# Order of the opening, block 0's transposes in two steps, and a new plan for the rest of a fused attention and feed-forward kernel

## The chip, the cores and the metric

The kernel runs on one core of a Trainium2 chip. A core has five engines that run on their own and wait for each other through semaphores: TensorE (PE, matmuls; PEld is its weight load, which overlaps), VectorE (DVE), ScalarE (ACT), GpSimd (POOL) and SyncE (SP, which here only issues DMA transfers). The metric is the device time of one execution in microseconds; lower is better. A chip's run of the same kernel repeats within some tenths of a per cent.

## The reference

The input x has 2048 rows of 576 columns in bf16. All of it is one layer with two branches that share a layer norm:

```
xn = layernorm(x)
q, k, v = split(xn @ wqkv)              # 32 heads of 18 columns
p = softmax(mask(q @ k.T * 18**-0.5))   # a row sees itself and the 255 rows before it
s = (p @ v) @ wo
h = sigmoid(xn @ w_gate) * (xn @ w_up)  # 4608 columns
g = silu(h @ w_down)
out = x + s * g
```

## The kernel before

**Tiles and stages.** The rows are worked in four stages (chunks) of 512 rows, each of four blocks of 128. In a stage: layer norm of the blocks, transposed copy `xnT` (columns on partitions), the query and key projection (`build_qk`), v (`build_v`), scores, exp and mask per head group (`build_attn`), probabilities times v (`build_pv`), output projection (`build_wo`), gate and up products for 36 tiles of 128 feed-forward columns (`gate_up` in `build_ffn`), their tanh and multiply (`tail`), and the down product (`down`). 576 columns are 64 + 4 x 128: `xnT` has five column blocks, of which block 0 holds the first 64 columns twice (the "doubled columns": `ln:dup`, L561, copies them next to the normalised row). All matmuls run in pairs on the two halves of TensorE's rows, by the helper `pair` (L127): one 64-row product for gate, one for up, at the same time. A gate/up tile has a first half of four column blocks (`f10`, 8 matmuls) and a second half of five (`f11`, 10 matmuls, which need the doubled block and the remainder weights `wgr`).

**The opening.** In stage 0 x comes by four DMAs of 144 KB (`load_x`) on SP's queue, ahead of the first weights: gate and up of the first group of two tiles (`wgs`, 256 KB each), their remainders (`wgr`, 64 KB each), the next group, and so on. Block by block, `build_ln` does the statistics on DVE (L541 to L547; for the third block on ACT, L600 to L604), the power for 1/sqrt on POOL (L549), the normalise (L557) and the doubled copy (L561) on DVE, ten small transposes on TensorE (L613) into PSUM and one evacuating copy to `xnT` (L590; on ACT for blocks 0 to 2, on DVE for block 3, `XE_ENG`). While TensorE has no data, `warm` gives it products of zeros: 43 pairs of 128 columns at the start and ten after the first transposes (`NWARM`). The first two gate/up tiles (`NEARLY = 2`) are done in four parts of one block each (`PARTS`), so that they can start when block 0 is there.

**What sets the order.** Nothing is ordered by hand. `build_graph` lists operations with their dependences, engine, estimated duration and priority. `schedule` is a list planner: it walks through a modelled time, and on each engine takes next the operation with the earliest modelled start (plus 10 ns per priority step), takes PSUM units for it from pools (`pool_s`, `pool_f`, `pool_v`), and so fixes each engine's instruction order; `emit` writes it out with semaphore waits. On the chip each engine keeps that order whatever the real times are. Constants such as `SPACE_NS` (least distance of score products), `DMA_ISSUE_NS` and the DMA slack model the chip.

**Runs.** `build_pv` makes eight runs of products of probabilities with v (L817), two per stage: 384 instructions in some 2.3 us (256 in stage 0). TensorE's instructions come from memory in blocks of 256. `fits` lets a run start only where, by the plan's times, the block boundaries in it have `FETCH_NS` between an instruction 320 places ahead and the boundary; otherwise the run is put off.

Of the kernel before, what the change touches and what calls it, by code (L numbers as in the profile page):

```python
# [7 lines left out]
S = 2048  # L8
D = 576
# [36 lines left out]
FETCH_NS = (6200.0, 4350.0)  # L46
RUN_NS = 6.3
STEP_NS = (54.0, 30.6)
# [21 lines left out]
X_PRIO = (0, 0, 0, 0)  # L70
# [4 lines left out]
XE_ENG = ("ACT", "ACT", "ACT", "DVE")  # L75
NWARM = (43, 10)
NEARLY = 2
FIRST_SLACK_NS = (-800.0, -1500.0)
BUSY_SLACK_NS = 1500.0
PARTS = (((0, 1), (1, 2), (2, 3), (3, 4)),) * NEARLY  # L80
# [10 lines left out]
POOL_IN_NS = 140.0  # L91
DMA_PE_NS = 690.0
FILL_NS = 100.0
SPACE_NS = (1700, 1800, 1700, 1700)
# [62 lines left out]
class Pool:  # L157
# [12 lines left out]
    def pick(self, n, now, barred=()):  # L170
        free = []
        for u in self.units:
            if u in barred:
                continue
            h = self.last[u]
            if h is None:
                free.append((0.0, self.units.index(u), u))
            elif h.rel and all(r.idx >= 0 for r in h.rel):
                free.append((max(now, max(r.end for r in h.rel) + self.late), self.units.index(u), u))
# [4 lines left out]
        return max(g[0] for g in got), sorted(g[2] for g in got)  # L184
# [11 lines left out]
class Op:  # L196
    __slots__ = ("eng", "est", "deps", "fn", "name", "prio", "start", "end", "tok", "needs_tok",
                 "nbytes", "slack", "idx", "succs", "cidx", "odeps", "acq", "lane", "filler", "space", "ni", "run", "then")

    def __init__(self, eng, est, fn, name, deps, prio, nbytes, odeps, acq):  # L200
# [33 lines left out]
        self.then = None  # L234
        for d in self.odeps:
# [23 lines left out]
class Builder:  # L259
# [40 lines left out]
    def alloc_memory(self):  # L300
# [61 lines left out]
        self.pool_f = Pool("F", [2, 3, 1], last)  # L362
        self.pool_v = Pool("V", [0, 1, 2, 3], last)

    def build_graph(self):
# [16 lines left out]
        self.op_xnT = [[] for _ in range(NC)]  # L382
        self.op_v = {}
# [34 lines left out]
    def load_x(self, c, i=0):  # L418
        if c == 0:
            for i in range(BPC):  # L420
                self.x_dma[i] = (self.dma(self.x0[:, i, :], self.x[i * P:(i + 1) * P, :], P * D * 2, f"dma:x{i}", ("x0", i), prio=X_PRIO[i]),
                                 self.x0[:, i, :])
                self.x_dma[i][0].slack = -220.0
# [20 lines left out]
    def load_rem(self, dst, srcs, name, lane, prio, deps=()):  # L444
        return [self.dma(dst[ROWS[1 - t], :], src[0:RD, :], RD * src.shape[1] * 3, name, lane + (t,), deps=deps, prio=prio)
                for t, src in enumerate(srcs)]

    def build_consts(self):
# [15 lines left out]
        self.warm(NWARM[0], z, None, 107)  # L464
# [25 lines left out]
    def warm(self, n, dep, before, est):  # L490
        h, zero = self.warm_h, self.warm_src

        def f_warm(eng):
            return pair(eng, self.halves(h, P), lambda r, t: zero[r, :],
                        lambda r, t: zero[r, :], True, True)
        for i in range(n):
            w = self.op("PE", est, f_warm, f"warm:{i}", deps=[dep], prio=4, acq=None if before else h, odeps=[before], ni=4)
            w.filler = h
            h.release(w)
            before = w  # L500
# [24 lines left out]
    def build_ln(self, c):  # L525
# [3 lines left out]
        for i in range(BPC):  # L529
# [49 lines left out]
            h = self.pool_s.hold()  # L579

            def f_tr(eng, h=h, sn=sn):
                return self.transposes(eng, h, lambda r, o: self.xnr[r, sn, o:o + P])
# [759 lines left out]
```

## Time and profile before

| what | us |
|---|---|
| median of three runs | 556.4 (556.1 to 556.68) |
| the profiled execution's own time | 556.48 |
| its span, first to last instruction | 555.2 |
| TensorE busy | 549.9 |
| first gate/up product starts | 7.98 |
| last TensorE work ends | 552.7 |

TensorE is the full engine, so idle time of the others costs nothing by itself. Times in the views count from the span's start. In a row of the timeline the first number is the start, the second the length of the group, xN the number of instructions in it; in brackets stand the idle time before it and what ended it. A pair of matmuls of n columns takes n / 2.4 + 2.7 ns at the full pace: 56 ns for 128 columns, 216 ns for 512.

### The profile page before, as it was taken

What the parts mean: (1) busy time and instruction counts of PE and PEld (TensorE: products, weight loads), DVE (VectorE), ACT (ScalarE), POOL (GpSimd) and SP (SyncE); (2) the same over time, 40 slices, a digit from 0 to 9 for tenths busy, and PEclk for the clock granted to TensorE, in tenths of its full rate; (3) what the DMA queues carried; (4) which work ended last, traced back from release to release, by engine and by line L of the source; (5) the groups of instructions that cost most, each with busy time, mean ns of one, the idle gap of its engine ahead of it and who ended that gap; (6) DMA issues with size and microseconds to landing.
All of it is one profiled execution on the core that took longest, in us unless ns stands there. A gap on an engine that the chain in (4) does not pass through costs nothing.

```text
span 555.2 us, 19412 instructions
## 1 busy us (share of the span) xinstructions
PE 549.9 (99%) x8342; PEld 341.2 (61%) x8342; DVE 325.1 (59%) x782; ACT 271.7 (49%) x379; POOL 208.8 (38%) x360
## 2 busy tenths in 40 slices
PE   8999999999999999999999999999999999999998
PEld 7454455777555655577855565447877655445887
DVE  5467677745966545746565557664455657653511
ACT  4246554432566543645265563764165555765021
POOL 5634353826271230554452322745063332700300
DMA  8899999542256664462126653663013464540001
GB/s 230 234 263 239 248 241 257 150 91 59 72 164 182 198 167 132 129 161 53 32 65 193 201 162 101 185 179 87 9 34 103 119 204 138 153 134 2 20 28 46
DMA packets 141213, 75.87 MB, mean 137 GB/s; under 512 B 43676, under 2 KB 139260, under 8 KB 141128
## 3 DMA queue, kind: packets, MB, share of 16 engines
q1 hardware_dynamic: 133704, 68.71, 47.3%
q0 software_dynamic: 7424, 5.92, 4.0%
q8 instruction: 66, 1.08, 0.8%
q14 instruction: 19, 0.16, 0.1%
HBM read 63.18 MB, written 2.36 MB: 118 GB/s over the span
## 4 chain that ended last, share of the span: by engine, by line
PE 98%; DMA 1%; SPq 0%; issue 0%; DVE 0%; ACT 0%
PE ps L127 95%; PE ps L817 3%; DMA wgs<-in_B_w_up_dram 1%; SPq L290 0%; ACT thf L1087 0%; PE ps L613 0%; DVE thf L1089 0%; DVE xf L1092 0%
## 5 line engine op out<-in xcount | busy, mean ns | idle before, releaser
L127 PE MATMUL ps<-xnT,wgs 64*128 64x512 bf16 (+1 forms) x2400 | 284.0, 368 | 0.6 <-DMA wgs<-in_B_w_up_dram 0.5
L767 ACT ACTIVATE expr<-ps 128x1024 bf16<-128x1024 f32 (+4 forms) x160 | 155.0, 968 | 81.0 <-PE ps L127 80.5
L127 PEld LDWEIGHTS ps<-xnT,wgs 64*128 64x128 bf16 x2400 | 114.7, 94 | 108.6 <-issue 1.1
L127 PE MATMUL ps<-wd_sb,hT 64*128 64x288 bf16 (+2 forms) x2448 | 152.7, 276 | 0.0
L290 POOL DMA_DIRECT2D qk<-qd x160 | 82.9, 524 | 161.7 <-PE ps L127 152.9
L977 DVE SCALAR_TENSOR_TENSOR hT<-tring,ps 128x512 bf16<-128x512 bf16 x144 | 98.6, 685 | 74.2 <-ACT tring L974 72.6
L974 ACT ACTIVATE tring<-ps 128x512 bf16<-128x512 f32 x144 | 86.2, 598 | 113.9 <-PE ps L127 112.3
L127 PEld LDWEIGHTS ps<-wd_sb,hT 64*128 64x128 bf16 x2448 | 113.0, 94 | 29.4
L780 DVE TENSOR_TENSOR expr<-expr,mask 128x128 bf16<-128x128 bf16 (+2 forms) x240 | 65.2, 299 | 62.0 <-ACT expr L767 59.4
L290 POOL DMA_DIRECT2D oT<-o2T x72 | 36.8, 520 | 115.3 <-DVE ot L848 52.4
L731 POOL TENSOR_SCALAR kx<-kprev,small 128x256 bf16<-128x256 bf16 x64 | 60.1, 949 | 6.0 <-PE ps L127 5.1
L127 PE MATMUL ps<-qk,kx 64*128 64x320 bf16 (+1 forms) x704 | 59.2, 254 | 0.0
L127 PE MATMUL ps<-xnT,wgr 64*128 64x512 bf16 (+1 forms) x300 | 56.0, 367 | 0.0
L127 PEld LDWEIGHTS ps<-qk,kx 64*128 64x128 bf16 x704 | 31.9, 94 | 26.6
L127 PE MATMUL ps<-xnT,wqg 64*128 64x512 bf16 (+1 forms) x320 | 37.7, 355 | 0.0
L652 DVE CAST qd<-ps 128x1024 bf16<-128x1024 f32 (+1 forms) x20 | 22.3, 1115 | 11.1 <-PE ps L127 11.1
L845 DVE STREAM_TRANSPOSE ot<-ps 128x512 f32<-128x512 f32 x32 | 20.3, 687 | 13.9 <-PE ps L817 13.8
L127 PEld LDWEIGHTS ps<-xnT,wgr 64*128 64x128 bf16 x300 | 15.0, 94 | 16.4
L731 DVE TENSOR_SCALAR kx<-qk,small 128x512 bf16<-128x512 bf16 x64 | 21.9, 370 | 5.4 <-PE ps L127 4.9
L853 DVE STREAM_TRANSPOSE o2T<-o 128x512 bf16<-128x512 bf16 x32 | 22.6, 706 | 3.0 <-DMA oT<-o2T 2.5
L127 PEld LDWEIGHTS ps<-xnT,wqg 64*128 64x128 bf16 x320 | 15.0, 94 | 11.5 <-issue 0.4
L1080 ACT ACTIVATE thf<-ps 128x576 bf16<-128x576 f32 x12 | 7.8, 650 | 27.4 <-PE ps L127 27.4
(68 smaller groups left out, 289.3 us busy)
## 6 DMA issues: line engine op xcount, KB each, us to landing
wgs<-in_B_w_gate_dram SPq DMA_DIRECT2D x72, 256.0 KB, 3.5
wgs<-in_B_w_up_dram SPq DMA_DIRECT2D x72, 256.0 KB, 4.0
wd_sb<-in_B_w_down_dram SPq DMA_DIRECT2D x9, 576.0 KB, 6.7
wqg<-in_A_wqkv_dram SPq DMA_DIRECT2D x32, 128.0 KB, 3.8
qk<-qd POOLq DMA_DIRECT2D x100, 36.0 KB, 2.7
wgr<-in_B_w_gate_dram SPq DMA_DIRECT2D x36, 64.0 KB, 3.1
wgr<-in_B_w_up_dram SPq DMA_DIRECT2D x36, 64.0 KB, 2.9
wvo<-in_A_wqkv_dram SPq DMA_DIRECT2D x4, 576.0 KB, 4.2
```

What stands on the lines that cost most here:

```text
L127: res = eng.matmul(outs[i], lhs(ROWS[t], i), rhs(ROWS[t], i), start=start, stop=stop, tile_position=(64 * t, 0))
L290: o = self.op(eng, DMA_ISSUE_NS[eng], lambda e: e.dma_start(dst, src), name, deps, prio, nbytes=nbytes)
L652: return eng.tensor_copy(dst, self.both(h, n))
L731: return e.tensor_scalar(self.kx[:, sx, pos:pos + n_ // SW, t, :], src.rearrange("p (s k) -> p s k", k=SW), self.half[:, t:t + 1], None, A ...
L767: return eng.activation(self.expr[:, se, :, lo * SW:NT], self.both(h, NT)[:, :, lo * SW:NT], ACTF.Exp, scale=SM_SCALE)
L780: return eng.tensor_tensor(e_, e_, m_, ALU.mult)
L817: res = eng.matmul(outs[i][p0:p0 + VH, cols], self.v_aug[ROWS[i], o:o + VH], self.expr[ROWS[i], se, t, cols], start=m == 0, stop=m == len( ...
L845: return e.transpose(self.ot1[:, p1, :], self.halves(hp, NT, un)[i])
L853: t2 = op("DVE", dve_ns(NT), lambda e, p2=p2, p3=p3: e.transpose(self.o2T[:, p3, :], self.o2[:, p2, :]), f"ot2:{c}:{pr}:{i}", deps=[on, d3 ...
L974: th = op("ACT", act_ns(NT), lambda e: e.activation(self.tring[:, st, :], bank(h, 0), ACTF.Tanh, scale=0.5), f"th:{c}:{ft}", deps=[pg, dt_ ...
L977: mu = op("DVE", dve_ns(NT), lambda e: e.scalar_tensor_tensor(self.hT[:, ft, :], self.tring[:, st, :], 1.0, bank(h, 1), ALU.add, ALU.mult) ...
L1080: th = op("ACT", act_ns(w), lambda e: e.activation(v2(t), y2(), ACTF.Tanh, scale=0.25), f"fth:{nm}", deps=[f2, dt_], prio=0)
```

## The change

Four things are changed together.

1. The fourth x block's DMA gets a lower priority and stands behind gate, up and both remainders of the first weight group on SP's queue.
2. Blocks 0 to 2 are transposed in two steps with PSUM units of their own (`pool_m`, `pool_r`): first the four blocks of plain columns, which wait for the normalise alone, then the doubled block, which waits for `ln:dup`. Each step has its own evacuating copy, on the engine in `XE_ENG` and `XR_ENG` (block 0 on DVE, blocks 1 and 2 on ACT). First halves of gate/up tiles need the first copy alone; second halves, query/key and v need both (`op_xnR`).
3. The warm-up is 44 pairs, all ahead of the first transposes; there are none behind them. The third gate/up tile is done early too, in two parts: blocks 0 to 2 together, then block 3 (`NEARLY = 3`, `PARTS`).
4. The planner's model is changed: arrival times of the opening's DMAs (`lat`), several latencies, `SPACE_NS`, and the test for a run. The test now takes as the trigger of a boundary's fetch the instruction 272 places ahead; the trigger counts from when the place 48 further ahead is reached, and not before any wait on another engine up to it is over (`held`). Three values of `FETCH_NS` stand for stage 0, the others, and the ends of the gate/up work, and the demand is relaxed as a run waits.

The order that follows on the engines: TensorE does 88 warm-up matmuls (86 before), block 0's 8 and 2 transposes, the first halves of tiles 0 and 1 for block 0 (16 matmuls), block 1's 8 transposes, tile 0's second half, block 1's 2 transposes, tile 1's second half, then block 1's products; block 2's transposes stand behind tile 0's first half for block 1. Tile 2's first half for three blocks follows, block 3's ten transposes, tile 2's second half, and the parts of block 3. DVE has block 0's two copies ahead of the normalise of block 1, and block 3's statistics behind the normalise of block 2. Behind the opening all engines' orders differ in many places, with the same operations; the last 30 operations of TensorE, DVE, ACT and SP are the same.

```diff
-FETCH_NS = (6200.0, 4350.0)
+FETCH_LEAD = 16
+QUEUED = 48
+FETCH_NS = (7800.0, 5900.0, 4250.0)
+RELAX_NS = 150e3
...
-X_PRIO = (0, 0, 0, 0)
+X_PRIO = (0, 0, 0, 1.8)
...
-XE_ENG = ("ACT", "ACT", "ACT", "DVE")
-NWARM = (43, 10)
-NEARLY = 2
-FIRST_SLACK_NS = (-800.0, -1500.0)
+XE_ENG = ("DVE", "ACT", "ACT", "DVE")
+XR_ENG = ("DVE", "ACT", "ACT")
+NWARM = ((44, 1),)
+NEARLY = 3
+OPEN_NS = 2000.0
+OPEN_BYTES_PER_NS = 256.0
+X_LAT_NS = (400.0, 600.0, 900.0, 800.0)
+W_LAT_NS = (650.0, 1100.0)
...
-PARTS = (((0, 1), (1, 2), (2, 3), (3, 4)),) * NEARLY
+PARTS = (((0, 1), (1, 2), (2, 3), (3, 4)),) * 2 + (((0, 3), (3, 4)),)
...
-FILL_NS = 100.0
-SPACE_NS = (1700, 1800, 1700, 1700)
+FILL_NS = 160.0
+SPACE_NS = (1900, 1800, 2000, 1800)
...
+        self.pool_a = Pool("F", [0], last)
+        self.pool_m = Pool("S", [0], last)
+        self.pool_r = Pool("S", [1], last)
...
-            h = self.pool_s.hold()
-
-            def f_tr(eng, h=h, sn=sn):
-                return self.transposes(eng, h, lambda r, o: self.xnr[r, sn, o:o + P])
-            tr = op("PE", KB * 29.5, f_tr, f"tr:{st}", deps=[ap, dup, self.op_ident, war], prio=0, acq=h, ni=20)
+            apart = i < BPC - 1
+            steps = ((range(1, KB), [ap, war], XE_ENG[i], self.pool_m), (range(1), [dup], XR_ENG[i], self.pool_r)) if apart else (
+                (range(KB), [ap, war, dup], XE_ENG[i], self.pool_s),)
+            for w, (ks, after, eng, pool) in enumerate(steps):
+                n, h = len(ks), pool.hold()
+
+                def f_tr(eng, h=h, sn=sn, ks=ks):
+                    return self.transposes(eng, h, lambda r, o: self.xnr[r, sn, o:o + P], ks)
+                tr = op("PE", n * 29.5, f_tr, f"tr:{st}:{w}", deps=[after, self.op_ident], prio=0, acq=h, ni=4 * n)
+
+                def f_xe(e, h=h, i=i, ks=ks):
+                    dst = self.xnT[:, xs, ks[0]:ks[-1] + 1, i * P:(i + 1) * P].rearrange("p k (t c) -> p t k c", t=2)
+                    src = self.tr_src(h)[:, :, ks[0]:ks[-1] + 1, :]
+                    return e.activation(dst, src, ACTF.Copy) if e is self.nc.scalar else e.tensor_copy(dst, src)
+                xe = op(eng, dve_ns(n * P, 1.9) if eng == "DVE" else act_ns(n * P), f_xe, f"xe:{st}:{w}", deps=[tr], prio=0)
+                h.release(xe)
+                if w == 0:
+                    self.op_xnT[c].append(xe)
+                if w or not apart:
+                    self.op_xnR.append(xe)
             self.r_xn.release(sn, tr)
-            if i == 0:
-                self.warm(NWARM[1], None, tr, 80)
...
-            xin = self.op_xnT[c][b0:b1]
+            xin = self.op_xnT[c][b0:b1] + (self.op_xnR[b0:b1] if half and not c else [])
...
-                        ahead = self.pool_f.hold()
+                        ahead = self.pool_a.hold()
...
-    def fits(self, at, n, st, places, ffn):
+    def fits(self, at, n, st, places, now, rate, waited):
         def when(p):
             if p < at:
-                return next(t0 + (p - a0) * w for a0, t0, w in reversed(places) if a0 <= p)
-            return st + TURN_NS + min(p - at, n) * RUN_NS + max(p - at - n, 0) * STEP_NS[ffn]
+                return next((t0 + (p - a0) * w, kind) for a0, t0, w, kind, held in reversed(places) if a0 <= p)
+            return st + TURN_NS + min(p - at, n) * RUN_NS + max(p - at - n, 0) * rate, now
         edge = at + (FETCH_AT - at) % FETCH
         while edge - FETCH - FETCH_AHEAD < at + n:
-            if edge > at and when(edge) - when(edge - FETCH - FETCH_AHEAD) < FETCH_NS[ffn]:
+            p = edge - FETCH - FETCH_LEAD
+            t0, kind = when(p - QUEUED)
+            for a0, _, _, _, held in reversed(places):
+                if a0 < p - FETCH:
+                    break
+                if a0 <= p:
+                    t0 = max(t0, held)
+            if p >= at:
+                t0 = max(t0, st)
+            if edge > at and when(edge)[0] - t0 < FETCH_NS[kind] * (1.0 - waited / RELAX_NS):
                 return False
             edge += FETCH
         return True
...
+                if o.lat is not None:
+                    moved = max(moved, stt + o.est + 700.0) + o.nbytes / OPEN_BYTES_PER_NS
+                    o.end = moved + o.lat
```

## The prediction

> **What bounds the kernel now.** The page's first part comes first: which engine is full, and how full.
>
> ```profile
> span 555.2 us, 19412 instructions
> PE 549.9 (99%) x8342; PEld 341.2 (61%) x8342; DVE 325.1 (59%) x782; ACT 271.7 (49%) x379; POOL 208.8 (38%) x360
> ```
>
> TensorE is busy for 549.9 of 555.2 us and no other engine passes 61%. The changed program holds the same 8342 matmuls: two more in the warm-up before the first transpose (88 for 86), 20 fewer behind it, and one more feed-forward tile cut in two (18 more). So time can only go where TensorE is not fed. The chain that ended last, in order of time, says where that is.
>
> ```profile
> 2.66 0.43 SPq L290
> 3.10 0.04 issue
> 3.14 4.71 DMA wgs<-in_B_w_up_dram
> 7.84 0.14 issue
> 7.98 1.00 PE ps L127 x26
> ...
> 86.18 2.07 PE ps L127 x17
> 88.25 0.05 issue
> 88.30 48.51 PE ps L127 x696
> ...
> 336.28 1.48 PE ps L817 x100
> 337.75 0.09 issue
> 337.84 1.06 PE ps L817 x77
> ```
>
> The first real product starts at 7.98, when the first up-projection weights have landed. From there to 552.7 the chain is TensorE, with two small breaks: at 88.25 and inside a run of probabilities x V (L817) at 337.75. Only 8 us ahead of the first product and about 1 us of small breaks can be won; the end (552.7 to 555.2) keeps its order. The timeline of the opening shows the activation side.
>
> ```profile
> 5.30 0.18 DVE L561 COPY xnr<-xnr 128x64 bf16<-128x64 bf16 x1
> 5.54 0.32 PE L613 MATMUL ps<-ident,xnr 64*128 64x64 bf16 x10 [0.33 <-DVE xnr L561]
> 5.69 0.72 PE L127 MATMUL ps<-hT 64*128 64x128 bf16 x20
> 6.49 0.68 ACT L590 ACTIVATE xnT<-ps 128x640 bf16<-128x640 bf16 x1
> 7.18 0.32 PE L613 MATMUL ps<-ident,xnr 64*128 64x64 bf16 x10 [0.76 <-DVE xnr L561]
> 7.54 0.70 ACT L590 ACTIVATE xnT<-ps 128x640 bf16<-128x640 bf16 x1 [0.37 <-PE ps L613]
> ```
>
> Block 0 of x is in xnT at 6.49 + 0.68 = 7.17, 0.7 us before the weights. The second block is transposed at 7.18, in the pause before the weights.
>
> **The change, part by part.** The sum is made against the profiled execution: span 555.2, time 556.48, so 1.28 us lie around the span; the median of three runs is 556.4, 0.08 less.
>
> *The fourth x block behind the first weights (X_PRIO).* On SP, gate and up move ahead by one x issue, 0.43 + 0.04 us; 147 KB less stand before them. The stretch from 5.1 to 8.0 us moved 262 GB/s at a DMA share of 0.97, so 147 KB are 0.56 us: landing 7.28 instead of 7.84. The up load's last pieces also linger: with those ahead of it, it closes 1.11 MB, but by 7.84 the queues had moved about 1.55 MB (the one-microsecond windows, summed). Loads of that tile took 4.2 to 4.9 us from issue to landing, the first up load 4.7; at 4.2 it would land 0.5 earlier. I take half, 0.25, so a landing at 7.03 and a first product 0.14 later, at 7.17: **0.81 us won**. Bounds: nothing won, if lingering pieces and not the bytes ahead set the landing; at most 1.7, at 6.3, where the activations stop it (next part).
>
> *Doubled columns apart, the first copies to DVE (XE_ENG, XR_ENG).* Block 0's eight transposes of whole columns wait for the normalise (ends 5.26), not for the copy behind it (5.48). DVE is free at 5.78; its 640-column evacuation at 10.62 took 0.49, so 512 columns are some 0.43: xnT ready at 6.2, for 7.17. Alone it wins nothing, as the weights are later. Its price is in the order: transposes of block 1 now stand behind the first 16 products and the pause before the weights no longer hides them: 10 matmuls, **0.15 us**. From its first transpose to a finished copy takes 0.36 (7.18 to 7.54), then some 0.60 on ACT for 512 of 640 columns (0.70), then about 0.05: 1.0 us. TensorE has in between 4 pairs at 0.03, 5 at 0.056, 1 at 0.03 and 5 at 0.056: 0.71. **A new wait of 0.28**. For block 2 the same count gives 0.93 of work for 1.0: **0.06**. With ACT as copier, its 0.19 us accumulator read ends at 6.59, so ACT itself is free.
>
> *A third tile cut early (NEARLY 3, PARTS).* Its two halves cost 9 more pairs, 0.0027 each: 0.02. The second half follows its first with only block 3's transposes (0.15) between; where before a second half follows its first with nothing between, at 87.2, 16 + 2 matmuls and the break show a wait of 0.23 beyond the pairs' 0.216. So **0.08**. Two things may come late here. Block 3: x3 now closes the same 1.25 MB that the first pair of remainder loads (wgr) closed; DVE gets to its statistics about 8.3, behind the copy at 8.09; they and the rest (aggregate, power, normalise, copy) take 2.5 us by the rows of 5.70 to 9.88, so transposes by 10.9; TensorE arrives at 7.17 + 4.3 = 11.5. Covered by 0.6, and the evacuation behind eight 0.06 us memsets by about 0.5. The second weight group, issued 4.95 and 5.59, lands 4.2 to 4.9 later (by 10.5); TensorE needs it at 7.17 + 3.65 = 10.8, two microseconds earlier in its work than before. Covered by 0.3; a start at 6.3 would lose up to 0.5 of its gain here.
>
> *Warm-up.* One pair more ahead, ten fewer behind the first transposes (0.72 us in a pause): nothing, unless the clock falls (rival 2).
>
> Before, 13 pairs from 7.98 to the transposes at 8.80 took 0.82 instead of 0.73: about 0.1 that the new order drops. Opening: -0.81 + 0.15 + 0.28 + 0.06 + 0.08 + 0.02 - 0.10 = **-0.32**.
>
> *Runs and all later order (fits, FETCH_NS, SPACE_NS, pools).* Everything behind is planned anew. What it can remove: the pause in the run at 336.21, which takes 2.69 us where its like at 457.60 takes 2.47 (0.22); the wait at 88.2 (0.23); and single waits of about 0.1 at 190.5 and 427. Together 0.65. What it adds: one place where a tile's second half follows its first directly (third tile of the second stage), 0.23; and new small waits of the kind that the old plan had. The old plan's unforeseen ones sum to 0.4, so I take 0.25 for them. **-0.17**, between -0.65 and +0.6. Weight loads in the first stage keep several microseconds between landing and use in both SP orders, and SP's and POOL's moved issues (wd, qk, oT) stand no later against their users; the cover is the ring of four weight slots. Waits by other engines cost nothing while TensorE goes on.
>
> Sum: 556.48 - 0.32 - 0.17 = 556.0; less 0.08 to the median, **555.9**.
>
> **Rivals.** *1. The weights come when the bytes say.* Without lingering pieces the landing is no later than the chain of x, and the first product starts at 6.4 instead of 7.17: 0.77 more, of which 0.3 may go to the second weight group; with the later breaks mostly gone (0.4 more): 555.9 - 0.77 + 0.3 - 0.4 = 555.0, between 554.5 and 555.3. For it: the queue moved 1.55 MB while 1.11 were asked first. Against: one late piece is enough, and every load in the opening shows one.
>
> *2. The clock falls back (slower).* Now TensorE rests from the transposes of block 0 (5.7) to the weights, 1.5 us in one piece with no narrow pairs in it. A cold start is in the trace: 62 matmuls in the 3.33 us from 1.00, a pair per 107 ns, then 56 ns. If it came again at the first product, 3.3 x (1 - 56/107) = 1.6 us are lost, on top of whichever start: 557.5, or 557.8 with the start at 7.42. [...] Against: rests of 0.5 and 0.8 us here left the pace at 56 ns. [...]
>
> *3. The change does not do what it says at the start.* The lingering piece comes at 7.8 whatever stands ahead, and the new waits in the opening stay: 556.4 + 0.49 - 0.17 = 556.7.
>
> *4. Instruction blocks come late in the runs.* The page's queue 8 brings 66 blocks of 16 KB; the 0.22 pause is one that came late. In the third stage the new order leaves 5.2 us of pair time ahead of that boundary, not 6.1. If the latency were fixed that costs 0.9 more: 556.8, with rival 3 557.6.
>
> **How the numbers follow.** Forecast 0.42 (own range 555.3 to 556.5), rival 1 0.30, rival 3 0.13, rival 2 0.08, rival 4 or other new waits 0.07. 0.2% is 1.1 us, about what a measurement of this kernel can tell from no change. Faster (below 555.3) is rival 1 and an edge of the forecast, 0.32; slower (above 557.5) most of rival 2 and half of rival 4, 0.13; same the rest. Range: from 554.7, inside rival 1, to 557.2, which leaves out rival 2's and part of rival 1's ends.
>
> **What would show it.** First product between 6.4 and 7.4, released by a DMA; ACT's copy of block 1 as releaser of a 0.3 wait after it; eight L817 runs, the longer ones all near 2.47. Wrong if pairs take 107 ns behind the first product, if the second weight group or block 3 appears as a releaser, or if breaks beyond the opening sum to over 1.3 us.

## The result and the profile after

The changed kernel is slower: 559.96 us (558.8 to 562.03), against 556.54 (556.1 to 556.81) for the kernel before on the same chip; ratio 1.0064, 95% interval 1.0053 to 1.0074. Forecast were 555.9 and a range of 554.7 to 557.2. A second set of runs gave 561.05 (559.16 to 562.70), ratio 1.0068, interval 1.0051 to 1.0086. Its times spread over more than 3 us, those of the kernel before over 0.7 to 1.5. One execution of the kernel before, at 970.94 us with a mean granted clock of 0.557, is left out here and in all that follows.

The profiled execution took 559.96 with a span of 558.7; before, 556.48 and 555.2. The page's first part, for TensorE:

```profile
span 558.7 us, 19419 instructions
PE 550.9 (99%) x8342; PEld 341.2 (61%) x8342; DVE 323.6 (58%) x784; ACT 271.5 (49%) x380; POOL 210.1 (38%) x360
```

The work is the same (8342 matmuls), so the 3.5 us lie in places where TensorE is not fed. The chain that ended last, in order of time (start, duration, what):

```profile
6.18 0.55 DVE xnT L607 x2
6.73 0.35 DVE xnr L572
7.08 0.62 PE ps L135 x16
7.70 0.12 PE ps L633 x8
7.82 1.07 issue
8.89 0.46 PE ps L135 x10
...
146.63 0.32 PE ps L135 x2
146.95 0.26 issue
...
216.12 1.47 PE ps L837 x99
217.59 0.26 issue
217.86 1.06 PE ps L837 x78
...
336.88 1.52 PE ps L837 x104
338.40 1.25 issue
339.65 1.02 PE ps L837 x64
...
460.54 1.47 PE ps L837 x99
462.01 0.48 issue
462.49 1.06 PE ps L837 x78
```

The first product comes 0.9 us earlier than before (7.08 for 7.98). Then "issue" stands where there was none: 1.07 us behind the second transposes, and one pause at or in four runs of probabilities x V (L837; in the kernel before one run had 0.09). "issue" is time in which TensorE waited for nothing that the profile shows. Measured from the start of one group of matmuls to the next, less their full-clock spacing, the four come to 0.44, 0.40, 1.40 and 0.61, 2.85 us in all, against 0.22 before.

To compare the openings whatever their order, I add up the products worked off by 20.0 us, each at its full-clock spacing in these traces (0.056 us for 128 columns, 0.163 for 384, 0.216 for 512; the one on its way at 20.0 counts in part): 11.53 us of products in the kernel before, 10.97 in the changed one. So the opening lost 0.56 in this execution, and the rest lost 2.9.

### The profile page after: what moved, and what is told of

The parts are those of the page before. It is cut to its first block, busy times and chain, and to the rows that moved or that the text cites. A ratio compares the mean times of both kernels' runs of the same rounds, so it can differ in the third digit from the quotient of the medians.

```text
span 558.7 us, 19419 instructions
## 1 busy us (share of the span) xinstructions
PE 550.9 (99%) x8342; PEld 341.2 (61%) x8342; DVE 323.6 (58%) x784; ACT 271.5 (49%) x380; POOL 210.1 (38%) x360
## 4 chain that ended last, share of the span: by engine, by line
PE 99%; issue 1%; DVE 0%; ACT 0%
PE ps L135 95%; PE ps L837 3%; PE ps L633 0%; DVE xnT L607 0%; DVE xnr L572 0%; ACT thf L1107 0%; DVE thf L1109 0%; DVE xf L1112 0%; DVE hT L471 0%; DVE small L472 0%
## 5 line engine op out<-in xcount | busy, mean ns | idle before, releaser
L800 DVE TENSOR_TENSOR expr<-expr,mask 128x128 bf16<-128x128 bf16 (+2 forms) x240 | 63.5, 292 | 75.3 <-ACT expr L787 74.2
L837 PE MATMUL ps<-expr,v_aug 64*19 64x320 bf16 (+4 forms) x1408 | 19.0, 254 | 1.9 <-issue 1.9
```

What stands on the lines that cost most here:

```text
L800: return eng.tensor_tensor(e_, e_, m_, ALU.mult)
L837: res = eng.matmul(outs[i][p0:p0 + VH, cols], self.v_aug[ROWS[i], o:o + VH], self.expr[ROWS[i], se, t, cols], start=m == 0, stop=m == len( ...
```

## Experiments

All orders are the planner's for the changed kernel (or for the kernel before, where that is said). Where instructions are taken away or added, the planner's count is set off by as many, so that the order stays. A "satisfied wait" is a wait of TensorE on a count that was reached long ago; two of them make one instruction (48 are 24 instructions in a_both's trace, 80 are 40 in d_nofill's), and the expectations count such instructions, not single waits. In the traces each takes TensorE 0.106 us. "The instruction 320 ahead" is the one 320 places ahead of a block's first, from which `fits` of the kernel before counts. Blocks are the 16 KB of instructions that the page's queue 8 brings (66 packets of 16,384 bytes). Each holds 256 of TensorE's instructions: the pauses at 217, 338 and 462 us of the changed kernel's trace stand 3840 instructions apart, 15 x 256. A block's start and landing are read from that queue's packets in the trace. A run of 192 pairs takes 2.40 us where nothing stops it; what it takes beyond that is called its pause. Beside each profile, each execution has its mean granted clock on record. It is 0.997 in the six profiled executions in which the clock is at 0.50 for a while and 1.00 in the other ten, so 0.997 or less marks a fall of the clock where there is no profile.

**First: is it the place of the blocks' boundaries?**

```
a_warm43:  NWARM = ((43, 1),)          # and 8 satisfied waits ahead of f10:0:8
a_shift20: 40 satisfied waits ahead of f10:0:8 (20 instructions)
a_both:    NWARM = ((43, 1),)          # and 48 satisfied waits ahead of f10:0:8
b_late20:  (kernel before) NWARM = (43, 5)   # 20 instructions fewer
```

> Theory A (instruction blocks): the pause of 1.07 us at 7.82 comes from the 16 KB instruction block that is fetched from 6.09 on instead of 7.69, and the pauses inside the runs from boundaries of blocks that stand too far into the run. Theory B (order and loads): the new order of x and weights makes one piece of the up remainder late whatever TensorE's instructions do, and the runs pause since the new order has weight loads in the queues there. This kernel is the changed one with 43 narrow pairs ahead of the transposes instead of 44; four satisfied waits are added to TensorE's stream in the first stage, so that every later instruction keeps its place in its block, and the order is the same. A: the first block's fetch starts near 7.7 again, the break after the first 16 products falls from 1.07 to 0.3 or less (what is then left is the wait on ACT's copy of block 1), and the time is 0.7 to 1.0 us below the changed kernel's 559.96, about 559.1; the four pauses in the runs stay. B: the break stays near 1.1 and the time within 0.2 of the changed kernel's.

Measured: 559.43 (558.39 to 560.47), ratio 1.0049, interval 1.0037 to 1.0061. The break at 7.82 went, but the first block now started at 10.06 instead of 6.09, behind the loads, and a new break came at its first instruction. TensorE's timeline:

```profile
6.58 0.68 PE L135 MATMUL ps<-xnT,wgs 64*128 64x128 bf16 x16 [0.49 <-DVE xnT L607]
7.08 0.29 PE L633 MATMUL ps<-ident,xnr 64*128 64x64 bf16 x8
7.54 0.40 PE L135 MATMUL ps<-xnT,wgs 64*128 64x128 bf16 x8 [0.17 <-issue]
...
10.19 0.33 PE L135 MATMUL ps<-xnT,wgs 64*128 64x128 bf16 x5
12.28 0.27 PE L135 MATMUL ps<-xnT,wgs 64*128 64x128 bf16 x3 [1.76 <-issue]
```

Theory A's half on the opening is borne out as far as the first break goes, not in its gain.

> Same two theories. The changed kernel, with 20 satisfied waits added to TensorE's stream in the first stage behind 28 us; the order is the same, and every block boundary behind them falls 20 instructions earlier in its run (209 instead of 229 in two of the gate/up stages' runs, 229 instead of 249 in the third, 240 instead of 260 in the one at 147 us). 20 instructions are 20 x (54 - 6) ns = 0.96 us more between a block's trigger and its first use. A: the pauses of 0.44, 0.40 and 0.61 go, that of 1.40 falls to about 0.45, the down stages' runs may show up to 0.1 at their second boundaries; the added waits cost below 0.2; the time is 2.2 us below the changed kernel's, about 557.8. The opening's pause of 1.07 stays. B: the pauses stay where they are, and the time is the changed kernel's or up to 0.2 above.

Measured: 560.34 (557.41 to 561.11), ratio 1.0051, interval 1.0034 to 1.0068. Of the pauses only the one at 217 us went; those at 147, 338 and 462 stayed (0.21, 1.39 and 0.46), and the last two's blocks started 2.5 and 2.8 us behind the instruction 272 ahead of the boundary, where in the changed kernel it was 1.6 and 1.9. That instruction had come earlier; the start had not. Theory A, in this form, falls. And a thing came up that the changed kernel's own profile does not have: a clock of 0.50 between 8.97 and 12.38 us.

> The two edits before this together: 43 narrow pairs, and boundaries 20 instructions earlier in the runs. A: both gains, 3.0 us below the changed kernel's, about 557.0, so still not below the kernel before (556.5). B: 559.9 to 560.2.

Measured: 560.19 (559.77 to 560.58), ratio 1.0061, interval 1.0049 to 1.0073. Here the pause at 338 was gone altogether, and those at 147, 217 and 462 stood at 0.66, 0.51 and 0.72. With the same boundaries as in a_shift20, other pauses: it depends on something beside the place. Two losses are not of this theory: the clock of this profile is at 0.50 from 7.67 to 11.09, and the 24 wait instructions in a row (24.5 to 26.9) leave TensorE idle for 0.35.

> The kernel before, its order unchanged, with five narrow pairs fewer behind the first transposes (they lie in a pause), so that all block boundaries fall 20 instructions later in their runs (251 instead of 231, 231 and 232 in the gate/up stages; 245 to 250 instead of 225 to 230 in the down stages). No order, no load and no engine but TensorE's stream is changed. A: 0.96 us less lead in the gate/up stages: pauses of about 0.6, 1.2 and 0.2 at 217, 338 and 459 us where there were 0, 0.2 and 0, and up to 0.2 in a down stage's run; time 1.5 to 2.2 us above the kernel before, about 558.4. B: within 0.3 of the kernel before, 556.5.

Measured: 557.56 (556.43 to 559.09), ratio 1.0018, interval 1.0009 to 1.0026. In the order of the kernel before, 20 instructions alone cost 1.0 us, about half of what was expected. In the profiled execution (557.37) the pause at 338 is 0.55, for 0.22 before, the down stage's run at 268.7 has a new one of 0.82, that at 459 one of 0.06, and 217 none. The place counts, but it is not the whole. The five narrow pairs were not free either: the two slowest of the eleven executions (558.84 and 559.09) have a mean clock of 0.997; the other nine have a median of 557.37.

**Second: what the blocks stand behind.** In the changed kernel's traces the blocks of the three runs started 0.32, 0.17 and 0.05 us behind the landing of a 256 KB weight load that was issued 3.2, 3.1 and 3.4 us ahead of that start. Since these loads land 0.7 to 0.8 us apart, that alone shows little. So:

```
c_hold:     dma:w:1:16, dma:w:2:12, dma:w:3:8 wait for the last product ahead of the run
c_wide:     NWARM = ((11, 4),)   # and 8 satisfied waits ahead of each of 33 gate/up products
c_widehold: both
c_x3first:  X_PRIO = (0, 0, 0, 0)
```

> Theory A of the runs before (the boundary's place in the run alone sets the pause) has not held: with 20 instructions more lead the fetches started later, not earlier. Theory C: a block that is fetched waits in line behind the weight loads that were issued just ahead of its request, and starts when their burst ends; the pause is set by the load. In the changed kernel a pair of 256 KB loads is issued at 212.28, 334.11 and 456.69, next to the requests of the blocks used at 217.9, 339.7 and 462.5. This kernel is the changed one, in which these three pairs (weight groups 16, 12 and 8 of stages 1, 2 and 3) wait for the last product ahead of the run, so they are issued some 3 to 4 us later; they are needed 10 us behind that. Nothing else is changed. C: these three blocks start within 2.9 us of the instruction 320 ahead of the boundary (4.2 to 4.5 in the changed kernel), the pauses of 0.40, 1.40 and 0.61 go, and the time is 2.0 to 2.5 us below the changed kernel's 559.96, about 557.6. The pause at 147 us and the opening stay. A: pauses as before, time 560.0; if the held loads come late for their products, slower still.

Measured: 560.0 (558.8 to 560.65), ratio 1.0053, interval 1.004 to 1.0066; the profiled execution 559.21. In the runs the pauses fell from 0.40, 1.40 and 0.61 to 0, 0.45 and 0, some 2 us, as theory C has it. But the blocks started 3.6, 3.5 and 4.1 us behind the instruction 320 ahead, not within 2.9. And the median did not follow, since the opening of the profiled execution had 9.63 us of products by 20 us, 1.3 less than that of the changed kernel, for one and the same code up to there: its clock was at 0.50 again.

> The opening. Seen so far: with 44 narrow pairs the first block is fetched at 6.09, and a piece of the up remainder lands 2 us behind the others (break of 1.07 and 1.08 us in two kernels); with 43 the remainder is in time, but the block is fetched at 10.06 or 10.43, behind the loads, and TensorE stands for 1.76 or 0.35 us at its first instruction. Theory C says that both are one queue: block and loads stand in one line, and whichever is behind is late. This kernel has the warm-up in 11 pairs of four times the width (the same 44 x 128 columns), so 132 instructions fewer ahead of the transposes, and the first boundary falls 132 instructions later, to about 16 us; 132 satisfied waits in the first stage (four ahead of each of 33 gate and up products) give them back, so that the later blocks stand as in the changed kernel. C: the up remainder is no longer late and no block is waited for ahead of 20 us; the breaks of the opening shrink by 1.0 us or more: 558.9. Runs as in the changed kernel. Rival: the late piece is the queue's own (every load of the opening has one) and stays whatever is fetched: 559.9 or more, with up to 0.5 for the added waits.

Measured: 560.06 (559.29 to 560.14), ratio 1.0054, interval 1.0042 to 1.0066; the profiled execution 559.29. The up remainder came in time (by 7.53), and the products follow each other from 6.90 with breaks of 0.16 and 0.19 us at most. 11.93 us of products by 20 us: 0.96 more than in the changed kernel and 0.40 more than before. That is near the gain that the prediction gave the opening (0.32), but in one execution: c_widehold, with the same opening, has 11.57. The median shows none of it; with two medians of the changed kernel 1.1 us apart, it could not tell a gain of 0.7.

Over the profiled executions of the changed order the late piece is clear. The last of the up remainder's 16 pieces landed at 8.69 to 9.11 in the five in which the first block started between 5.91 and 6.78 (44 narrow pairs ahead of the transposes), 0.9 to 1.9 us behind the 15th; in the eight variants of the changed kernel in which it started at 8.48 or later, at 7.16 to 7.77. A block is not the only thing that makes a piece late: in the profile of the kernel before the piece came at 8.35, 1.0 behind the 15th, with the block at 7.69. Nor does every block: in b_late20, with a block on its way from 6.92 to 8.91, the piece came at 7.56, 0.06 behind the 15th.

> Both edits before this: wide warm-up and the three held pairs of loads. C: the gains add, 3.1 to 3.6 us below the changed kernel's, about 556.6, level with the kernel before (556.56), as what is then left of new breaks is 0.44 at 147 us, 0.23 and 0.2 in single waits, against a start 0.9 us earlier. A: 559.9.

Measured: 559.0 (558.27 to 559.53), ratio 1.0037, interval 1.0025 to 1.0049; the profiled execution 558.27, with pauses of 1.1 at 338 us, none at 217 and 462, and a new wait of 0.3 on a load at 101 us. About 1 of the 3.4 us is back, not all.

> The changed kernel with one part undone: the fourth x block is loaded ahead of the first weights again (the second and third blocks' transposes then move ahead of the products that stand there; all other work, the runs and their boundaries stay). If the order of x is worth what the first products showed (7.98 in the kernel before, 6.58 to 7.36 in four of the new ones), the first product comes at 7.6 to 8.0 and the time is 0.5 to 0.9 above the changed kernel's, 560.5 to 560.9. If what the order wins at the start is lost again in the breaks behind it, the time is within 0.3 of 559.96.

Measured: 561.19 (559.04 to 562.11), ratio 1.0071, interval 1.0054 to 1.0088. The first product came at 7.26, not at 7.6 to 8.0. The order of x is worth 0.1 to 0.5 us at the start (four profiles of the changed kernel's opening start at 6.74 to 7.12), not 0.8, and the time can't be told from the changed kernel's. (The start of the kernel before also varies: 7.98 in its profile, 7.31 and 7.79 in two variants with the same loads.)

**Third: the clock.**

```
d_fill:   NWARM = ((2, 4), (36, 1))                          # same columns
          if i == 0: self.warm(6, 3, None, tr, 54)           # behind the first transposes
d_nofill: (kernel before) NWARM = (43, 0)                    # and 80 satisfied waits later
d_all:    d_fill's pairs, NWARM = ((11, 4),), c_hold's waits, a_shift20's boundaries
```

> The clock. In the profiles of three variants of the changed kernel whose opening is its own or nearly so, the granted clock drops to 0.50 at 8.6 to 8.9 us and comes back at 11.6 to 12.8, after TensorE rested 1.2 to 1.4 us before the first product and 1.1 to 1.5 us behind the second transposes; in the profile of the changed kernel itself it stays at 1.00 with rests of 1.1 and 1.1. Theory E: the changed kernel sits at the edge, falls in part of its executions, and this is most of the spread of its times (558.8 to 562.0). This kernel is the changed one with six pairs of 3 x 128 columns behind the first block's transposes, in the rest before the first product, and a warm-up of two pairs of 4 x 128 and 36 of 128 columns ahead (the same 44 x 128 columns, the same number of instructions in all, the same order). E: the clock is 1.00 throughout; the times draw together, the highest below 560.5 and the median 0.3 to 1.0 below 559.96; the breaks in the runs stay. Rival: the spread comes from the blocks in the runs; the times spread as before, median 559.7 to 560.3.

Measured: 559.28 (558.84 to 560.82), ratio 1.0052, interval 1.0039 to 1.0065. Clock 1.00 throughout, 11.64 us of products by 20 us. The median is 0.7 below the first set's and 1.8 below the second's; the highest time is not below 560.5. None of its five executions has a mean clock below 1.00, and their times still spread over 2.0 us; nor is the clock most of the changed kernel's spread, as theory E had it, since its executions at 1.00 run from 558.8 to 562.03. This chain also shows, uncovered, the wait on ACT's copy that the prediction had priced at 0.28:

```profile
7.89 0.14 PE ps L636 x8
8.03 0.02 issue
8.05 0.61 ACT xnT L607
8.66 0.05 issue
8.71 0.40 PE ps L135 x8
```

By TensorE's own starts it is 0.27 here and in the three later kernels with these pairs.

> The same theory in the kernel before: the ten narrow pairs behind its first transposes are taken away (40 satisfied waits in the first stage keep all later boundaries where they were; order unchanged). The rests are then about 1.2 to 1.4 us before the second transposes and 0.5 behind them. E: the clock falls to 0.50 for some 3 us in part or all of the executions, at 1.6 us each; median 556.5 to 558.2 with a spread of over 1.5 us, where the kernel before spreads over 0.7 to 1.3. Rival (the pairs did nothing): 556.5, spread as before, clock 1.00.

Measured: 558.2 (557.03 to 558.69), ratio 1.0024, interval 1.0015 to 1.0033. The median is 1.7 above the kernel before, but not all of that is the clock. Four of the eleven executions have a mean clock of 0.997, with a median of 558.4; the other seven have 557.4, still 0.9 above the kernel before. In the trace the added wait instructions would account for that: each of the two groups of 20 in a row (from 27.6 and from 32.3 us) leaves TensorE idle for 0.4 (at 29.2 and 34.1), 0.8 in all. So without the ten narrow pairs the clock falls in part of the executions, which are then about 1.0 us slower than the rest. The windows of the opening, one us each (stretch, sum, then TensorE, weight loads, DVE, ACT, POOL; the third figure from the end is the granted clock):

```profile
6.00:7.00 1.00, 0.00 (x0) 0.00 (x0) 1.00 (x3) 1.00 (x3) 0.85 (x3) 1.00 0.91 252
7.00:8.00 1.00, 0.53 (x18) 0.44 (x20) 0.69 (x4) 0.47 (x2) 0.45 (x1) 1.00 0.90 246
8.00:9.00 1.00, 1.00 (x33) 0.93 (x28) 0.40 (x3) 0.37 (x1) 0.48 (x1) 0.69 0.95 284
9.00:10.00 1.00, 1.00 (x30) 1.00 (x26) 0.74 (x6) 0.64 (x1) 0.26 (x2) 0.50 0.96 285
10.00:11.00 1.00, 1.00 (x24) 1.00 (x21) 0.13 (x4) 0.07 (x1) 0.94 (x2) 0.50 0.94 266
```

TensorE rested 1.5 us ahead of the second transposes and 0.3 behind them; then the clock halved; with 0.60 in the next window the four lose 0.31 + 0.50 + 0.50 + 0.40 = 1.7 us, 3.4 us at half. By 20 us 1.4 of it is left (10.13 us of products for 11.53), as the first product came 0.2 earlier.

> All remedies in the changed kernel's order: the wide warm-up (first boundary 108 instructions later), the six pairs behind the first transposes, the three held pairs of loads, and boundaries 20 instructions earlier in the runs (209, 229, 209, and 240 in place of 260 at 147 us). With only wide warm-up and held loads the median was 559.0 and the profiled execution, 558.3, still had pauses of 1.1 at 338 and 0.4 at 147. If blocks and loads are the whole of it, these go, the down stages' runs pay up to 0.3, the clock stays at 1.00, and the time is 557.0 to 557.6. If the new order costs something of its own beside them, 558.3 or more.

Measured: 558.3 (557.44 to 559.08), ratio 1.0028, interval 1.0016 to 1.0041; pauses of 0.45 and 1.05 remained at 147 and 338.

**Fourth: what is left in the runs, and the changed kernel's own clock.**

```
e_hold2:    d_fill, and dma:w:1:15, dma:w:2:11, dma:w:3:7 (and what follows on SP) wait likewise
f_hold2s20: e_hold2, and 40 satisfied waits ahead of f10:0:8
f_again:    the changed kernel
```

> With one pair of loads held, the blocks at 338 us still started only 1.1 to 1.35 us behind the last landing of the pair issued before that one; in stretches without loads a block starts 1.0 to 1.4 us behind the instruction 320 ahead of its boundary. Theory C then says that the pair before must be held as well. This kernel is the one with six pairs behind the first transposes (d_fill: median 559.28, pauses of 0.37, 1.27 and 0.93 in the three runs), boundaries where they were, and with both pairs of loads ahead of each of the three runs (groups 15 and 16, 11 and 12, 7 and 8 of stages 1, 2 and 3) waiting for the last product ahead of the run. C: the three blocks start 1.0 to 1.5 us behind the instruction 320 ahead (4.0 to 4.9 in d_fill), the three pauses go, and the time is 2.2 to 2.6 us below d_fill's, 556.7 to 557.1; up to 0.5 more if a held load comes late for its product. If instead the place of the boundary or the hold by DVE's buffer sets the pause, they stay, and the time is 559.3 or more.

Measured: 558.29 (557.72 to 559.44), ratio 1.0027, interval 1.0018 to 1.0037; the profiled execution 557.86, 1.09 below d_fill's. The chain:

```profile
8.97 1.78 PE ps L135 x58
10.76 0.95 issue
11.71 0.99 PE ps L135 x14
...
215.91 2.40 PE ps L840 x168
...
336.28 1.55 PE ps L840 x106
337.83 0.24 issue
338.07 1.02 PE ps L840 x64
...
458.96 2.40 PE ps L840 x168
```

Two of the three runs are whole again (2.40) and the third pauses for 0.4: 2.1 us back in the runs, near what was expected. Of this 0.7 was given away in the opening (10.90 us of products by 20 us, 11.64 in d_fill), where the first block, which started at 8.78 behind the loads and took 1.45, came late. But the blocks of the runs did not start 1.0 to 1.5 us behind the instruction 320 ahead; they started 3.4 to 3.7 behind it, with no load moving.

> With both pairs of loads held no load moved in the 3.4 us before the blocks of the three runs, two of the three pauses went, and the one at 338 us fell to 0.43; its block still started 3.45 us behind the instruction 320 ahead, and 1.03 us behind the release of the wait (on DVE's freeing of a buffer) 267 instructions ahead of the boundary. This kernel adds the 20 satisfied waits of the first stage to that one (e_hold2, median 558.29, profiled 557.86), so that every boundary falls 20 instructions earlier in its run. If the place of the boundary now sets the lead, as no load stands in the way, the blocks are requested 0.96 us earlier against the run and the pause at 338 goes. If the request stands behind that wait wherever the boundary lies, the start keeps its time against the run, and the pause is 0.43 + 20 x 6 ns = 0.55, with new ones of 0.1 in the other two. The opening may differ by 1 us either way, as it has from execution to execution; the verdict is read from the trace.

Measured: 558.84 (558.32 to 560.63), ratio 1.0034, interval 1.0021 to 1.0046. The boundary moved, the starts did not: 1.10, 1.32 and 1.11 us behind the release of the last wait on DVE that stands over 240 instructions ahead of the boundary (1.23, 1.03 and 1.22 in e_hold2): now 247 instructions ahead, and 267 there. The pause at 338 is 1.24 (block started 1.32 behind the release, moved for 1.31, first use 1.33 behind the landing), the other two runs have none, the place at 147 has 0.64, and a product at 221 us waited 0.85 for a load that stands behind the held ones. The second of the two readings holds for these runs.

> The changed kernel itself, unaltered, for another profiled execution and more times. Theory E (its opening sits at the edge of the clock's fall): the granted clock falls to 0.50 at 8.6 to 8.9 us in about half of the executions, at 1.7 us each, so times spread from 558.8 to 562 and the profile has an even chance of showing it. Without E: clock 1.00, times within 1 us of 559.96. In both cases the pauses at 147, 217, 338 and 462 us are there at 0.4, 0.4, 1.4 and 0.6, give or take 0.3.

Measured as above (561.05). The profiled execution, 561.74, has what the first profile lacks:

```profile
6.00:7.00 1.00, 0.43 (x18) 0.32 (x14) 0.82 (x3) 0.07 (x1) 0.92 (x3) 1.00 0.94 210
7.00:8.00 1.00, 0.48 (x22) 0.35 (x15) 0.70 (x4) 0.49 (x1) 0.48 (x1) 1.00 0.95 286
8.00:9.00 1.00, 0.00 (x0) 0.00 (x0) 0.16 (x1) 0.11 (x1) 0.00 (x0) 1.00 0.72 206
9.00:10.00 1.00, 0.80 (x21) 0.83 (x23) 0.58 (x2) 0.15 (x1) 0.00 (x0) 0.71 0.39 101
10.00:11.00 1.00, 1.00 (x29) 1.00 (x26) 0.60 (x3) 0.13 (x1) 0.25 (x1) 0.50 0.41 120
11.00:12.00 1.00, 1.00 (x24) 1.00 (x21) 0.61 (x2) 0.77 (x2) 0.30 (x1) 0.50 1.08 318
12.00:13.00 1.00, 1.00 (x26) 1.00 (x22) 0.27 (x8) 0.00 (x0) 0.93 (x1) 0.58 1.03 283
```

Rests of 0.8 and 1.9 us, then the clock at half from about 9.4 to 12.8: (0.29 + 0.50 + 0.50 + 0.42) = 1.7 us of clock lost. 9.11 us of products by 20 us, 2.4 less than before. The pauses at 147, 217, 338 and 462 are 0, 0.67, 1.32 and 0.61.

The half stretch is 3.41 us long here. Up to 5.7 us the narrow pairs of the warm-up still take 107 ns; the first at full pace is at 6.74. Cut where the trace's clock changes, the windows are:

```profile
6.01:9.42 3.41, 1.12 (x41) 0.92 (x36) 1.68 (x6) 0.65 (x2) 1.39 (x3) 1.00 0.81 219
9.42:12.83 3.41, 3.41 (x78) 3.41 (x74) 2.06 (x14) 1.04 (x3) 1.34 (x2) 0.50 0.76 217
```

All six profiles with a fall look like this: 3.41 us at full pace from the clock's rise (at 4.26, 4.97, 4.97, 5.45, 5.56 and 6.01 in a_both, c_hold, d_nofill, c_x3first, a_shift20 and here), then 3.41 at half. What tells them from the other profiles of this case is how much product time, at full spacing and without transposes, lies in the first 3.41 us: 0.56 to 1.00 where the clock fell; 1.16 in the kernel before, 1.22 or more in the others whose rise can be read, and 1.20 in a later stretch of a_warm43, where it held. Where it begins differs between executions of one kernel: in the changed kernel's first profile at 6.72, with 1.48 us of products in it, here at 6.01, with 0.67.

Over all executions, the clock fell in ten of 24 with the changed kernel's opening (changed kernel 5 of 12, a_shift20 1 of 7, c_hold 4 of 5), in none of 28 with the six pairs (d_fill and the three kernels built on it), in none of 10 with the wide warm-up (c_wide, c_widehold), and in none of 70 of the kernel before.

No variant of the changed kernel beat the kernel before; the nearest, e_hold2, has the ratio 1.0027.

## Why the prediction was wrong, point by point

*The start.* Right in size: 7.17 forecast, 7.08 measured. The releaser was to be a DMA; the profile names DVE, but the first up load's last piece had landed only at 6.83, and in c_wide and a_shift20, where the profile names that load, the first product also stands 0.25 behind its landing. The reason was partly wrong, and luck had a part: c_x3first, with the fourth block of x ahead of the weights again, started at 7.26, and the start of 7.98 that the gain was counted from was 7.31 and 7.79 in two other profiles with the old loads.

*"Warm-up. One pair more ahead, ten fewer behind the first transposes: nothing, unless the clock falls."* This is the step that failed in the opening, and both halves of it did.
- With the pair more the first block started 1.6 us earlier (6.09 for 7.69), next to the up remainder, whose last piece came at 8.80: the break of 1.07. With the block moved away by 43 pairs (a_warm43) or by the wide warm-up (c_wide) the break is 0.2 or less, which shows that the block's place makes the piece late here; b_late20 shows that a block beside loads need not do so.
- The ten pairs fewer let the clock fall, rival 2. It had a chance of 0.08, on the argument that rests of 0.5 and 0.8 us had left the pace at 56 ns. The trace of the kernel before has no longer one. That a rest of 1.5 us would leave it there too, as the forecast's sum has it, was the author's estimate, and with 1.5 and 0.3 the clock fell in d_nofill. The longest rest does not tell the falls apart in these traces: it was 1.9 us in f_again and 1.3 in a_shift20, where the clock fell, and 1.76 in a_warm43 (up to 12.28), where it held. In f_again the rests of 0.8 and 1.9 left 0.67 us of products in 3.41 us. Of four profiled executions with the changed kernel's opening three fell, of all 24 ten. Its price was right: 1.6 us forecast, 1.7 measured, and the five executions of the changed kernel with a fall have a median of 561.74, the seven without 559.96. d_nofill shows it in the kernel before, where the pairs were taken away; with six pairs put back (d_fill and the three kernels built on it) no execution has it. So the fall explains the slower executions and the second median, not the miss as such: without it the time is still 4 us above the forecast.

*ACT's copy of block 1, 0.28.* Right: 0.27 in d_fill and the three kernels built on it, and 0.12 in c_wide, behind another break of 0.16. In the changed kernel itself the break hid it.

*"Opening: -0.32."* Where neither a late piece nor the clock is in the way, single executions gained 0.40 (c_wide), 0.11 (d_fill) and 0.04 (c_widehold) and lost 0.06 (d_all): the sign is mostly right, the size can't be told, as b_late20, with the old opening, has 0.35 more than the kernel before. In the changed kernel it was +0.6 in one execution and +2.4 in the other.

*"Runs and all later order: -0.17."* The second step that failed, and the larger. The forecast let the pause of 0.22 in one run go; instead the pauses grew to 2.85 (+2.6). Rival 4 was the mechanism, with a price of 0.9 for one run and a shared chance of 0.07. It took the latency as fixed and looked at one boundary. The runs show three terms. From the release of the last wait ahead (on DVE or on TensorE's own products, 247 to 270 instructions before the boundary) a block took 1.0 to 1.3 us to its start where no load moved (e_hold2, f_hold2s20), 0.9 to 1.4 to move and 1.3 to 1.5 to its first instruction, about 3.4 in all (3.96 at f_hold2s20's pause at 338); with weight loads in the queues the start came at 1.75 to 2.1 in the changed kernel's profile, 0.5 to 1.0 more. In the kernel before the lead from that release to the boundary is 4.31, 3.86 and 4.29, with one pause of 0.22, at 3.86. In the new order it is 3.85, 2.80 and 3.86, and the pauses are 0.40, 1.40 and 0.61. That the loads are one part is shown (c_hold, e_hold2); that the wait is the other is shown for these three runs by f_hold2s20.

*The small terms.* The wait at 88.2 is gone, and the third tile of the second stage costs 0.23 (at 148.73), both as forecast; a wait of 0.2 at 220 on ACT is the kind of small new one that 0.25 had been set aside for. No product behind 20 us waited more than 0.15 for a weight in the changed kernel.

*Sum.* Against the profiled 556.48: +0.6 in the opening and +2.6 for the pauses are measured, and +0.3 is what then is left to 559.96. In the execution with the clock at half, 2.4 + 2.6 + 0.3 give 561.8 (561.74). Together these explain the forecast's miss of 4 us; the range missed because it gave the pauses in the runs, rival 4, 0.9 us in one run where three runs and the place at 147 lost 2.6 more. Its chance of 0.13 for slower is also more than its own parts give (at most 0.08 + half of 0.07, 0.115).

*What stays open.* Which instruction asks for a block. In the three runs its start follows the wait whether that stands 267 or 247 instructions ahead of the boundary, but elsewhere blocks have started less than 0.6 us behind, or ahead of, the release of waits at 240 to 271. Why the pause at 338 went in a_both and not in a_shift20, with the same boundaries. And whether c_wide's better opening lasts beyond one execution: the profiled one is the fastest of its five.

## What to carry to other kernels

A filler that looks idle may hold the clock up: without the ten narrow pairs it fell in four of d_nofill's eleven executions, with them in none of 70. Before such products in a pause are taken away, add up the product time that is left in any 3.4 us around it. Here 1.0 us or less went with a fall of the clock and 1.16 or more with none, and where the 3.41 us begin differs between executions (6.72 and 6.01 for one kernel). And instructions are a load too: where the trace shows instruction blocks on their way while the kernel works (66 of 16 KB here), find each in the trace, see which wait stands ahead of its start and which loads land just before it, and treat the time from that wait's release to the block's first instruction as a due time of the plan. In the three runs it was about 3.4 us where no load moved, and 4.2 to 4.5 (lead and pause) with weight loads in the queues in the changed kernel. The pauses at 147, 217, 338 and 462 us there, which the profile puts down to "issue", all stood at a block's edge.

## What the chip showed that was not expected

- The clock halved for 3.41 us (1.7 lost in f_again and d_nofill alike) behind 3.41 us at full pace that hold 0.56 to 1.00 us of product time, in all six profiles with a fall. The rests in them were 0.8 and 1.9 us (f_again), 1.2 and 1.3 (a_shift20) or 1.5 and 0.3 (d_nofill).
- One 16 KB block on its way beside the opening's loads (1.1 to 1.9 us for it) went with a delay of one of the 16 pieces of a load by 0.9 to 1.9 us in five profiles of the changed order, and not in b_late20; the load is as late as that piece.
- With weight loads in the queues the blocks of the three runs started 1.75 to 2.1 us behind the release of the last wait ahead of them (changed kernel), without them 1.0 to 1.3 (e_hold2, f_hold2s20). In the down stages of the changed kernel's trace about half of the 29 blocks start 1.0 to 1.5 us behind the instruction 320 ahead, the others later, up to 3.5.
- 132 instructions of satisfied waits on TensorE, four ahead of each product, cost no more than about 0.2 us in all (c_wide between 40 and 80 us: 0.17 more than the changed kernel). Twenty in a row cost 0.4 twice in d_nofill and nothing that the trace shows in a_shift20.
